# Attention and a two-layer feed-forward on one Trainium2 core: when the layout transfers are issued, and which engine subtracts in 2 of 18 steps

## Chip, cores and metric

One core of one Trainium2 chip runs the whole program. The metric is device time in microseconds of one execution; before the change three runs gave 998.31, 1001.68 and 1002.51 us, the median is 1001.68 us.

## What is computed

The reference, cut to what matters (4 batches, 8 heads, 1152 positions, head width 64; 2304 tokens, 512 to 2048 to 512):

```python
q_pool = q.reshape(B, H, S // 2, 2, D).mean(axis=3)
scores = scale * np.matmul(q_pool, k.transpose(0, 1, 3, 2))
scores = scores - np.max(scores, axis=-1, keepdims=True)
attn = np.exp(scores)
attn = attn / (np.sum(attn, axis=-1, keepdims=True) + 1e-09)
attn_out = np.matmul(attn, v)
x = attn_out.transpose(0, 2, 1, 3).reshape(B * S, H * D)
h = x @ w_in
r = np.maximum(h, 0.0)
out = (s * (r * r) + b) @ w_out
```

## The kernel before

The 32 heads are taken in 16 pairs. A head has 9 blocks of 128 keys, so a pair has 18 **steps**, numbered 0 to 17 here, and the attention 288. The feed-forward follows it in the last 417 us or so.

**A step.** `score_step` (line 480) makes the scores `s` of one block of keys against the head's 576 pooled queries: four matmuls on `kk` and `qq`. The kind of the step is read from the string `KIND`. In a "v" step ScalarE writes the exponential twice, once rounded (`ph`) and once in full, and VectorE subtracts them to `pl` (line 501). In a "g" step it is the same, but the full one goes to a buffer `pe` and GpSimd subtracts. In a "w" step (whole) there is one exponential, to `pe`, and nothing is subtracted. Three steps later `value_step` multiplies: for "v" and "g" six matmuls in rounded float32 (ph with vv, ph with vl, pl with vv, for two halves; lines 524, 526, 528), for "w" two matmuls in full float32 (pe with vf, line 518; each is two records in the trace). After a head's last block, `finish` lets ScalarE copy the sums out (lines 544 and 545, called clearing here), and the next head's first value matmuls need these banks. One or two matmuls `m` per step (line 456) find the maxima of the scores of a later pair.

**Preparing a pair.** For each head `load_v` fetches the values (`vf`), and `prep_v` lets GpSimd split them into `vv` and `vl`. For each pair `load_k` and `load_q` fetch keys and queries (`kraw`, `qraw`: 4 and 8 transfers), and `prep_pair` turns them: VectorE transposes, GpSimd adds (`qs`), rounds (`kh`, `qh`, `qz`) and subtracts (`kT`, `qT`). `lay` then issues five transfers for one head, two to `kk` and three to `qq`: the **layout transfers** ("l0" the first head, "l1" the second; lines 404 to 407). `shift` finds a head's maximum, and ScalarE sends it in two small transfers (`c` to `qq`, lines 471 and 472).

**What sets the order.** Each engine runs its instructions in the order written, and tables say at which step of a pair a piece is written: `PREP` for the pieces of preparation, `LR` for the k and q loads, `VS` for `prep_v`; the values are loaded at steps 3 and 12. Layouts, loads and results all go through SyncE's queue. In steps n % 18 == 4 from n = 166 on, weights of the feed-forward are fetched and, from pair 10 on, converted on ScalarE, VectorE and GpSimd (`conversions`, lines 163 to 180).

**Semaphores of the transfers.** The built program has eight for all transfers of SyncE and ScalarE, DMAHW0 to DMAHW7, given out in turn. A transfer waits until the one before it with the same semaphore has landed.

The line that the layouts' steps come from, and those that use it:

```python
            if p + 2 < NPAIR and n % 18 == PREP[0][1]:
                prep = prep_pair(p + 2)
            for name, at in PREP if n >= 8 else ():
                if n % 18 == at and name in prep:
                    prep.pop(name)()
```

Of the kernel before, what the change touches and what calls it, by code (L numbers as in the profile page):

```python
# [31 lines left out]
KB = 384  # L32


KIND = "vgvwvgvgw" * 2

PP = (("ka", 0), ("kb", 0), ("ha", 0), ("hb", 1), ("qs", 1), ("qt", 1), ("qm", 2), ("qh", 2), ("qz", 2), ("kl", 2), ("ql", 3), ("l0", 7))
PREP = (("qs", 9), ("ka", 10), ("kb", 11), ("ha", 11), ("qt", 12), ("hb", 12), ("kl", 12), ("qm", 13), ("qh", 13), ("qz", 13), ("ql", 14), ("l0", 0), ("l1", 8))
LR = 13
LD = 1  # L40
VS = (7, 16)
XT = (1, 2, 3, 4, 8)
# [10 lines left out]
def f32(ap):  # L53
    return ap.bitcast(F32)
# [3 lines left out]
def attention_moe_kernel(ctx: ExitStack, tc: tile.TileContext, q, k, v, w_in, w_out, s_in, b_in, out):  # L58
# [12 lines left out]
    NPAIR = NH // 2  # L71
# [138 lines left out]
    def hi_of(eng, out, in_):  # L210
        if eng is nc.scalar:
            nc.scalar.activation(out, in_, AF.Copy)  # L212
        else:
            eng.tensor_scalar(out=out, in0=in_, scalar1=1.0, scalar2=0.0, op0=ALU.mult, op1=ALU.add)  # L214
# [115 lines left out]
    qm = ap.tile([P, P], F32R, name="qm")  # L330
# [16 lines left out]
    def load_k(p):  # L347
        kraw[p] = ap.tile([P, NB, 32], F32, tag="kraw", name=f"kraw{p}")
        for r, b, h, c in quarters(p):
            nc.sync.dma_start(kraw[p][r], k[b, h, :, c].rearrange("(j t) i -> t j i", t=32))  # L350
# [11 lines left out]
    def load_v(hd):  # L362
        nc.sync.dma_start(vfs[hd % 2][:, :, 0:D], v[hd // H, hd % H].rearrange("(j p) d -> p j d", p=P))

    def prep_pair(p):

        kr, qr = kraw.pop(p), qraw.pop(p)
        kT = ap.tile([P, S], F32, tag="kT", bufs=2, name=f"kT{p}")
        qT = ap.tile([P, SQ], F32, tag="qT", bufs=2, name=f"qT{p}")
        qs = ap.tile([P, NBQ, 32], F32, tag="qs", name=f"qs{p}")  # L370
        kh = ap.tile([P, S], F32R, tag="kh", bufs=2, name=f"kh{p}")
        qh = ap.tile([P, SQ], F32R, tag="qh", bufs=2, name=f"qh{p}")
        krv = kr.rearrange("p j i -> p (j i)")
        lo, hi = slice(0, SQ), slice(SQ, S)

        def corner():
            assert holds.get("qm", -1) == p - 1
            for h in range(2):
                d = slice(h * D, (h + 1) * D)
                hi_of(nc.scalar, qm[d, d], qT[d, NT4 * P:])  # L380
            holds["qm"] = p

        def k_hi(part, last):
            hi_of(nc.scalar if p < 2 else nc.gpsimd, kh[:, part], kT[:, part])
            if last:
                khs[p] = kh

        def q_hi():
            hi_of(nc.scalar if p < 2 else nc.gpsimd, qh, qT)
            qhs[p] = qh  # L390

        def q_blocks():

            for h in range(2):
                r = slice(h * D, (h + 1) * D)
                hi_of(nc.scalar if p < 2 else nc.gpsimd, qzs[p % 2][r, h].rearrange("p (t m) -> p t m", t=NT4), qT[r, :NT4 * P].rearrange("p (m t) -> p t m", t=NT4))

        def lay(h):
            hd = 2 * p + h
            kk, qq = kks[hd % 3], qqs[hd % 3].rearrange("p i a n -> p i (a n)")  # L400
            r = slice(h * D, (h + 1) * D)
            ks = ((f32(kk[D:P, 0, :]), kT[r]), (f32(kk[0:D]), f32(kh[r]).unsqueeze(1).to_broadcast([D, 2, S])))
            for dst, src in ks[::-1] if hd == 0 else ks:
                nc.sync.dma_start(dst, src)
            nc.sync.dma_start(f32(qq[0:D, 0, :]), f32(qh[r]))
            nc.sync.dma_start(f32(qq[D:P, 0, :]), f32(qh[r]))
            nc.sync.dma_start(f32(qq[0:D, 1, :]), qT[r])
            holds["k", hd % 3] = hd

        return {  # L410
            "ka": lambda: nc.vector.transpose(out=kT[:, lo], in_=krv[:, lo]),
            "qs": lambda: (nc.vector if p < 2 else nc.gpsimd).tensor_tensor(out=qs, in0=qr[:, :, 0, :], in1=qr[:, :, 1, :], op=ALU.add),
            "kb": lambda: nc.vector.transpose(out=kT[:, hi], in_=krv[:, hi]),
            "ha": lambda: k_hi(lo, False),
            "qt": lambda: nc.vector.transpose(out=qT, in_=qs.rearrange("p j i -> p (j i)")),
            "hb": lambda: k_hi(hi, True),
            "qh": q_hi,
            "qz": q_blocks,
            "kl": lambda: nc.gpsimd.tensor_tensor(out=kT, in0=kT, in1=f32(kh), op=ALU.subtract),  # L419
            "ql": lambda: nc.gpsimd.tensor_tensor(out=qT, in0=qT, in1=f32(qh), op=ALU.subtract),  # L420
            "qm": corner,
            "l0": lambda: lay(0),
            "l1": lambda: lay(1),
        }
# [55 lines left out]
    def score_step(hd, j, kind):  # L480
        assert holds["k", hd % 3] == holds["c", hd % 3] == hd
        kk, qq = kks[hd % 3], qqs[hd % 3]
        ps = ps_s.tile([P, 2, 512], F32, tag="s", name=f"s{hd}_{j}")
        for a in range(2):
            for i in range(2):
                nc.tensor.matmul(ps[:, a, :HALF], kk[:, i, j * P:(j + 1) * P], qq[:, i, a], start=(i == 0), stop=(i == 1))  # L486
        if kind != "v":
            pe = late.tile([P, 2, HALF], F32, tag="pe", bufs=PE, name=f"pe{hd}_{j}")
        if kind == "w":
            nc.scalar.activation(pe, ps[:, :, :HALF], AF.Exp, scale=SCALE)  # L490
            prob[hd, j] = pe, None
            return
        ph = late.tile([P, 2, HALF], F32R, tag="ph", bufs=PB, name=f"ph{hd}_{j}")
        pl = late.tile([P, 2, HALF], F32R, tag="pl", bufs=PB, name=f"pl{hd}_{j}")
        nc.scalar.activation(ph, ps[:, :, :HALF], AF.Exp, scale=SCALE)  # L495

        full = ps[:, :, :HALF] if kind == "v" else pe
        nc.scalar.activation(full, ps[:, :, :HALF], AF.Exp, scale=SCALE)  # L498
        prob[hd, j] = ph, pl
        eng = nc.vector if kind == "v" else nc.gpsimd  # L500
        fresh.append(lambda: eng.tensor_tensor(out=pl, in0=full, in1=f32(ph), op=ALU.subtract))  # L501
# [92 lines left out]
    prep = prep_pair(0)  # L594
# [11 lines left out]
    for n in range(AHEAD):  # L606
# [3 lines left out]
        if n == 11:  # L610
            load_v(1)
            prep = prep_pair(1)
    nc.sync.dma_start(sb[:, 0:1], s_in.unsqueeze(0).to_broadcast([P, 1]))
    nc.sync.dma_start(sb[:, 1:2], b_in.unsqueeze(0).to_broadcast([P, 1]))

    moe = Moe()
    weights_a = conversions(wa, wstage, 0, SW[0], 1, STA)
    NS = NH * NJ

    for n in range(NS + LAG):  # L620
        hd, j = divmod(n, NJ)

        at = (n - LAG) % NJ if n >= LAG else None
        products = None
        units = iter(range((n + AHEAD) * NU // 18, (n + AHEAD + 1) * NU // 18) if n + AHEAD < NS else ())
        for part in ORD[at] if at is not None else "sff":
            if part == "s" and n < NS:
                score_step(hd, j, KIND[n % 18])
            elif part == "f":
                for u in units:  # L630
                    max_unit(u, ps_m, "m")
                    break
            elif part == "v":
                if products is None:
                    products = value_step(*divmod(n - LAG, NJ))
                next(products)
        for fn in fresh:
            fn()
        fresh.clear()
        if n < NS:  # L640
            p, h = divmod(hd, 2)
            for name, at in PP:
                if n == at:
                    prep.pop(name)()
            if n == LD:
                load_k(2)
                load_q(2)
            if p + 2 < NPAIR and n % 18 == PREP[0][1]:
                prep = prep_pair(p + 2)
            for name, at in PREP if n >= 8 else ():  # L650
                if n % 18 == at and name in prep:
                    prep.pop(name)()
            if p + 2 < NPAIR:
                if n % 18 == LR and p + 3 < NPAIR:
                    load_k(p + 3)
                    load_q(p + 3)
            if hd + 1 < NH:
                if j == LAG and hd >= 1:
                    load_v(hd + 1)
                if n % 18 in VS:  # L660
                    prep_v(hd + 1)
            if n == NS - 3 * NJ:
                moe.fetch(0)
            if n == NS - 2 * NJ:
                moe.split(0, 1)
            if (CB - n) % CP == 0 and 0 <= CB - n < 7 * CP:
                weights_a()
        tick()
# [79 lines left out]
```

## Time and profile before

| What | us |
|---|---|
| median of three runs | 1001.68 |
| the profiled execution | 1000.3 |
| its span in the trace | 998.4 |
| TensorE busy (matmuls) | 921.4 |
| VectorE, ScalarE, GpSimd busy | 630.1, 564.7, 549.8 |

The execution's own time is 1.9 us more than its span, and lies 1.4 us below the median. Busy times are sums over the span; matmuls overlap at their ends, so a busy TensorE is not one at its peak. The start of a step's first score matmul is the best clock of the attention: the 16 pairs begin at 22.1, 57.9, 92.5 and so on, pair 8 at 302.7, pair 10 at 370.8, pair 14 at 515.2.

### The profile page before, as it was taken

The page shows a single profiled execution, that of the slowest core. Times are in us where ns is not written, and L with a number is a line of the kernel's source. Part 1 is how long each engine was busy: PE and PEld are TensorE (multiplying, and loading weights), DVE is VectorE, ACT ScalarE, POOL GpSimd, SP SyncE. Part 2 cuts the span into 40 slices and gives each one's busy share as a digit, 9 for nine tenths or more (in the row PEclk, how much of TensorE's full clock was granted, in tenths as well). Part 3 has the DMA queues.
Part 4 walks back from the last instruction along what each step waited for, and adds up shares of the span by engine and source line. Part 5 has one row for each costly group of instructions (what it writes and reads, how often), then busy time and mean ns, then how long its engine had stood idle before and what let it go on. Part 6 is the DMA issues. An engine that isn't in the chain of part 4 may idle for free.

```text
span 998.4 us, 16537 instructions
## 1 busy us (share of the span) xinstructions
PE 921.4 (92%) x5776; PEld 821.1 (82%) x5776; DVE 630.1 (63%) x1168; ACT 564.7 (57%) x1086; POOL 549.8 (55%) x437
## 2 busy tenths in 40 slices
PE   5998988899899899888889998999999999999998
PEld 3887877788788788877778887789999899999997
DVE  5766776676676668668767556676767664334333
ACT  2776665666676667667667856564444443333332
POOL 7667647757755785786695766673534440010000
PEclk9999999999999999999999999999999999999999
DMA  8987865865686597578574135665354433222311
GB/s 151 174 160 138 173 130 94 175 146 105 131 169 129 103 192 162 108 155 179 108 165 118 46 110 166 201 218 163 127 169 127 148 106 106 64 67 89 99 43 43
DMA packets 255313, 131.18 MB, mean 131 GB/s; under 512 B 203776, under 2 KB 227328, under 8 KB 255232
## 3 DMA queue, kind: packets, MB, share of 16 engines
q1 hardware_dynamic: 244512, 129.62, 54.4%
q10 hardware_dynamic: 10720, 0.52, 0.7%
q8 instruction: 46, 0.75, 0.3%
q14 instruction: 35, 0.29, 0.1%
HBM read 68.68 MB, written 18.87 MB: 88 GB/s over the span
## 4 chain that ended last, share of the span: by engine, by line
PE 58%; POOL 13%; DMA 8%; ACT 8%; DVE 6%; issue 4%; ACTq 1%; SPq 0%; POOLq 0%; DVEq 0%
PE h L272 16%; PE y L299 16%; PE s L486 9%; PE o L524 4%; PE m L456 4%; POOL pl L501 4%; PE o L528 4%; PE o L526 3%; PE o L518 3%; POOL kT L419 2%; POOL qz L214 2%; DMA vf<-in_v_dram 2%; DMA kk<-kh 2%; ACT ph L495 2%; DMA wsto<-in_moe_w_out_dram 2%
## 5 line engine op out<-in xcount | busy, mean ns | idle before, releaser
L457 DVE TENSOR_REDUCE pm<-m 128x1 f32<-128x384 f32 x432 | 233.0, 550 | 128.8 <-PE m L456 124.6
L495 ACT ACTIVATE ph<-s 128x576 fp32r<-128x576 f32 x224 | 145.9, 651 | 133.7 <-PE s L486 114.1
L272 PE MATMUL h<-x,wih 128*128 128x256 f32 x1152 | 213.2, 283 | 6.2 <-DVE gl L286 3.9
L486 PE MATMUL s<-qq,kk 128*128 128x288 f32 x1152 | 213.8, 308 | 4.1 <-DVE pl L501 3.6
L272 PEld LDWEIGHTS h<-x,wih 128*128 128x128 f32 x1152 | 185.8, 189 | 21.2 <-DVE gl L286 3.5
L501 POOL TENSOR_TENSOR pl<-pe,ph 128x576 fp32r<-128x576 f32 x96 | 137.5, 1432 | 104.8 <-ACT pe L498 103.5
L486 PEld LDWEIGHTS s<-qq,kk 128*128 128x128 f32 x1152 | 174.7, 192 | 16.4 <-PE o L528 4.4
L272 PE MATMUL h<-x,wil 128*128 128x256 f32 x576 | 162.2, 282 | 0.0
L528 PE MATMUL o<-pl,vv 128*128 128x288 f32 x448 | 135.7, 303 | 27.4 <-POOL pl L501 27.4
L456 PE MATMUL m<-kh,qz 128*128 128x384 f32 x384 | 153.5, 409 | 5.9 <-DVE pm L457 5.8
L524 PE MATMUL o<-ph,vv 128*128 128x288 f32 x448 | 138.7, 310 | 12.0 <-issue 4.4
L253 POOL TENSOR_TENSOR x<-xr,x 128x1024 fp32r<-128x1024 f32 x27 | 64.8, 2401 | 152.6 <-ACT x L212 146.9
L280 DVE SCALAR_TENSOR_TENSOR h<-h,sb,r 128x256 f32<-128x256 f32 x144 | 70.2, 488 | 115.2 <-ACT r L289 115.2
L526 PE MATMUL o<-ph,vl 128*64 128x288 f32 x448 | 134.1, 299 | 5.4 <-POOL vl L431 5.2
L528 PEld LDWEIGHTS o<-pl,vv 128*128 128x128 f32 x448 | 85.7, 191 | 45.9 <-POOL pl L501 35.4
L289 ACT ACTIVATE r<-h 128x256 f32<-128x256 f32 x144 | 55.7, 387 | 111.0 <-PE h L272 111.0
L501 DVE TENSOR_TENSOR pl<-s,ph 128x576 fp32r<-128x576 f32 x128 | 96.3, 752 | 28.5 <-ACT s L498 21.3
L299 PE MATMUL y<-wol,gh 128*128 128x512 f32 x288 | 113.1, 393 | 0.0
L299 PE MATMUL y<-woh,gl 128*128 128x512 f32 x288 | 112.9, 392 | 0.0
L299 PE MATMUL y<-woh,gh 128*128 128x512 f32 x288 | 112.6, 391 | 0.0
L272 PEld LDWEIGHTS h<-x,wil 128*128 128x128 f32 x576 | 109.6, 190 | 0.0
L524 PEld LDWEIGHTS o<-ph,vv 128*128 128x128 f32 x448 | 85.6, 191 | 25.1 <-ACT l L545 8.0
(89 smaller groups left out, 1492.0 us busy)
## 6 DMA issues: line engine op xcount, KB each, us to landing
kk<-kh SPq DMA_DIRECT2D x32, 576.0 KB, 5.6
kraw<-in_k_dram SPq DMA_DIRECT2D x64, 144.0 KB, 3.7
vf<-in_v_dram SPq DMA_DIRECT2D x32, 288.0 KB, 4.8
kk<-kT SPq DMA_DIRECT2D x32, 288.0 KB, 3.3
qq<-qh SPq DMA_DIRECT2D x64, 144.0 KB, 5.6
xr<-xd SPq DMA_DIRECT2D x18, 512.0 KB, 4.0
qraw<-in_q_dram SPq DMA_DIRECT2D x122, 72.0 KB, 2.5
wsti<-in_moe_w_in_dram SPq DMA_DIRECT2D x16, 512.0 KB, 5.0
```

Of the source, the lines that this page charges most:

```text
L253: nc.gpsimd.tensor_tensor(out=xl, in0=xr, in1=f32(xh), op=ALU.subtract)
L272: nc.tensor.matmul(h[:, :TB], st[:, c, :], mv[:, c, :], start=(n == 0), stop=(n == 3 * NC - 1))
L280: nc.vector.scalar_tensor_tensor(out=t, in0=h[:, :TB], scalar=sb[:, 0:1], in1=r, op0=ALU.mult, op1=ALU.mult)
L299: nc.tensor.matmul(y[:, :DM], st[:, ts_], mv, start=(first and n == 0), stop=(last and n == 2))
L456: nc.tensor.matmul(ps[:, :KB], st, khs[p][:, e * KB:(e + 1) * KB], start=True, stop=True)
L457: nc.vector.tensor_reduce(out=pms[p][:, col, e:e + 1], in_=ps[:, :KB], axis=AX.X, op=ALU.max)
L486: nc.tensor.matmul(ps[:, a, :HALF], kk[:, i, j * P:(j + 1) * P], qq[:, i, a], start=(i == 0), stop=(i == 1))
L495: nc.scalar.activation(ph, ps[:, :, :HALF], AF.Exp, scale=SCALE)
L501: fresh.append(lambda: eng.tensor_tensor(out=pl, in0=full, in1=f32(ph), op=ALU.subtract))
L524: nc.tensor.matmul(o[:, :HALF], vv[:, j], ph[:, a], start=first, stop=False)
L526: nc.tensor.matmul(o[0:D, :HALF], vl[:, j], ph[:, a], start=False, stop=False)
L528: nc.tensor.matmul(o[:, :HALF], vv[:, j], pl[:, a], start=False, stop=last)
```

## The change

Two edits. In `KIND`, of nine steps the kinds are now v w v g v w v g w instead of v g v w v g v g w: of 18 steps 8 are "v" as before, 4 instead of 6 "g", 6 instead of 4 "w". The "g" steps are 3, 7, 12 and 16 instead of 1, 5, 7, 10, 14 and 16. In `PREP`, the layouts of the pair ahead are written at steps 4 and 13 instead of 0 and 8, and the k and q loads at step 14 instead of 13; a second dictionary, `lays`, keeps the layouts that fall after step 9, at which the next pair's preparation replaces `prep`.

```diff
-KIND = "vgvwvgvgw" * 2
+KIND = "vwvgvwvgw" * 2
...
-PREP = (("qs", 9), ("ka", 10), ("kb", 11), ("ha", 11), ("qt", 12), ("hb", 12), ("kl", 12), ("qm", 13), ("qh", 13), ("qz", 13), ("ql", 14), ("l0", 0), ("l1", 8))
-LR = 13
+PREP = (("qs", 9), ("ka", 10), ("kb", 11), ("ha", 11), ("qt", 12), ("hb", 12), ("kl", 12), ("qm", 13), ("qh", 13), ("qz", 13), ("ql", 14), ("l0", 4), ("l1", 13))
+LR = 14
...
+    lays = {}
...
-            if p + 2 < NPAIR and n % 18 == PREP[0][1]:
-                prep = prep_pair(p + 2)
-            for name, at in PREP if n >= 8 else ():
-                if n % 18 == at and name in prep:
-                    prep.pop(name)()
+            if n % 18 == PREP[0][1]:
+                lays = {k: prep[k] for k in ("l0", "l1") if k in prep}
+                prep = prep_pair(p + 2) if p + 2 < NPAIR else {}
+            for name, at in PREP:
+
+                ops = prep if name not in ("l0", "l1") or at < PREP[0][1] else lays
+                if n % 18 == at and name in ops and n >= 8:
+                    ops.pop(name)()
```

**SyncE, around the value load of a pair's second head** (pair 8; the number behind a name is its buffer's, and a row shows the semaphores that it waits for). Before, from the fifth q load on, and ScalarE's two sends of c that use DMAHW1 and DMAHW3:

```order
L358 DMA qraw_3595<-in_q_dram 32x18x32 [waits DMAHW0_49]
L358 DMA qraw_3595<-in_q_dram 32x18x32 [waits DMAHW1_49]
L358 DMA qraw_3595<-in_q_dram 32x18x32 [waits DMAHW2_49]
L358 DMA qraw_3595<-in_q_dram 32x18x32 [waits DMAHW3_49]
L404 DMA kk_94<-kT_3483 64x1152 [waits DMAHW4_49,PE_49,Pool_49]
L404 DMA kk_94<-kh_3486 64x2x1152 [waits DMAHW5_49,PE_49]
L405 DMA qq_97<-qh_3487 64x576 [waits DMAHW6_49,Pool_49]
L406 DMA qq_97<-qh_3487 64x576 [waits DMAHW7_49]
L407 DMA qq_97<-qT_3484 64x576 [waits DMAHW0_49,Pool_49]
L363 DMA vf_104<-in_v_dram 128x9x64 [waits DMAHW1_49,PE_49]
L471 DMA qq_99<-c_3752 1x128x4 [waits DMAHW1_49,DVE_49]
L472 DMA qq_99<-c_3752 1x64x1 [waits DMAHW3_49]
```

Now, from the third q load on; the two sends of c use DMAHW7 and DMAHW0:

```order
L358 DMA qraw_3491<-in_q_dram 32x18x32 [waits DMAHW6_49]
L358 DMA qraw_3491<-in_q_dram 32x18x32 [waits DMAHW7_49]
L358 DMA qraw_3491<-in_q_dram 32x18x32 [waits DMAHW0_49]
L358 DMA qraw_3491<-in_q_dram 32x18x32 [waits DMAHW1_49]
L358 DMA qraw_3491<-in_q_dram 32x18x32 [waits DMAHW2_49]
L358 DMA qraw_3491<-in_q_dram 32x18x32 [waits DMAHW3_49]
L363 DMA vf_104<-in_v_dram 128x9x64 [waits DMAHW4_49,PE_49]
L404 DMA kk_94<-kT_3358 64x1152 [waits DMAHW5_49,Pool_49]
L404 DMA kk_94<-kh_3361 64x2x1152 [waits DMAHW6_49]
L405 DMA qq_97<-qh_3362 64x576 [waits DMAHW0_49,Pool_49]
L471 DMA qq_99<-c_3615 1x128x4 [waits DMAHW7_49,DMAHW5_49,DVE_49]
L472 DMA qq_99<-c_3615 1x64x1 [waits DMAHW0_49]
```

The five layout transfers of the first head stood between the q loads and the value load, and now stand behind it. The sends of c come ahead of the q loads that use their semaphores: before, those were the sixth and the eighth; now they are the fourth and the fifth.

**GpSimd, the preparation of a pair** (pl is the subtraction of a "g" step; pl_1 and pl_5 before are those of steps 10 and 14, pl_3 now that of step 12, and pl_7 that of step 16). Before:

```order
L412 TENSOR_TENSOR qs_3485<-qraw_3168 128x576
L501 TENSOR_TENSOR pl_1_3497<-pe_1_3495,ph_1_3496 128x576
L214 TENSOR_SCALAR kh_3486<-kT_3483 128x576 x2
L419 TENSOR_TENSOR kT_3483<-kT_3483,kh_3486 128x1152
L214 TENSOR_SCALAR qh_3487<-qT_3484 128x576
L214 TENSOR_SCALAR qz_102<-qT_3484 64x512 x2
L501 TENSOR_TENSOR pl_5_3611<-pe_5_3609,ph_5_3610 128x576
L420 TENSOR_TENSOR qT_3484<-qT_3484,qh_3487 128x576
L501 TENSOR_TENSOR pl_7_3650<-pe_7_3648,ph_7_3649 128x576
L214 TENSOR_SCALAR vv_105<-vf_103 128x9x64
```

Now:

```order
L412 TENSOR_TENSOR qs_3360<-qraw_3080 128x576
L214 TENSOR_SCALAR kh_3361<-kT_3358 128x576
L501 TENSOR_TENSOR pl_3_3415<-pe_3_3413,ph_3_3414 128x576
L214 TENSOR_SCALAR kh_3361<-kT_3358 128x576
L419 TENSOR_TENSOR kT_3358<-kT_3358,kh_3361 128x1152
L214 TENSOR_SCALAR qh_3362<-qT_3359 128x576
L214 TENSOR_SCALAR qz_102<-qT_3359 64x512 x2
L420 TENSOR_TENSOR qT_3359<-qT_3359,qh_3362 128x576
L501 TENSOR_TENSOR pl_7_3526<-pe_7_3524,ph_7_3525 128x576
L214 TENSOR_SCALAR vv_105<-vf_103 128x9x64
```

One subtraction of step 12 stands between the two halves of kh where one of step 10 stood ahead of both, and none is left between qz and qT.

## Rows read from the trace of the kernel before

**Rows 1.** The page: TensorE's busy time and share of the span with the other engines', and the chain of work that ended last, by engine.

```profile
PE 921.4 (92%) x5776; PEld 821.1 (82%) x5776; DVE 630.1 (63%) x1168; ACT 564.7 (57%) x1086; POOL 549.8 (55%) x437
...
PE 58%; POOL 13%; DMA 8%; ACT 8%; DVE 6%; issue 4%; ACTq 1%; SPq 0%; POOLq 0%; DVEq 0%
```

**Rows 2.** Busy time by stage: pairs 1 to 9, and pairs 10 to 13. A row has the stretch, its length, then each engine's busy time and count, TensorE's granted clock, the DMA share and GB/s.

```profile
57.90:370.80 312.90, 280.07 (x1793) 249.61 (x1792) 214.84 (x388) 206.89 (x378) 209.66 (x171) 0.99 0.71 141
370.80:515.20 144.40, 128.00 (x799) 112.51 (x798) 106.53 (x188) 97.83 (x181) 106.86 (x87) 0.99 0.70 146
```

**Rows 3.** TensorE's timeline in pair 8 (302.7 to 337.8) and the first steps of pair 9: start, duration, line, output and inputs, count, and in brackets the idle time before it with what ended it. Each row of L486 is the score matmuls of one step: step 9 at 318.40, 10 at 319.89, 11, 12, 13 at 326.71, 14 at 329.38, 17 at 334.40, 0 at 337.79, 2 at 340.96, 3 and 4.

```profile
318.40 0.69 PE L486 MATMUL s<-qq,kk 128*128 128x288 f32 x4
...
319.36 0.29 PE L528 MATMUL o<-pl,vv 128*128 128x288 f32 x1
...
319.89 0.69 PE L486 MATMUL s<-qq,kk 128*128 128x288 f32 x4
...
321.56 0.69 PE L486 MATMUL s<-qq,kk 128*128 128x288 f32 x4
...
323.02 0.91 PE L486 MATMUL s<-qq,kk 128*128 128x288 f32 x4
...
324.51 0.40 PE L524 MATMUL o<-ph,vv 128*128 128x288 f32 x1 [0.41 <-POOL vv L214]
...
326.71 0.70 PE L486 MATMUL s<-qq,kk 128*128 128x288 f32 x4
...
329.38 0.69 PE L486 MATMUL s<-qq,kk 128*128 128x288 f32 x4
...
334.40 0.69 PE L486 MATMUL s<-qq,kk 128*128 128x288 f32 x4
...
337.15 0.40 PE L528 MATMUL o<-pl,vv 128*128 128x288 f32 x1 [1.62 <-POOL pl L501]
...
337.79 0.69 PE L486 MATMUL s<-qq,kk 128*128 128x288 f32 x4
...
340.96 0.69 PE L486 MATMUL s<-qq,kk 128*128 128x288 f32 x4
...
342.81 0.69 PE L486 MATMUL s<-qq,kk 128*128 128x288 f32 x4
...
345.13 0.69 PE L486 MATMUL s<-qq,kk 128*128 128x288 f32 x4
```

**Rows 4.** GpSimd's timeline in pair 8, from the subtraction of step 7 to that of step 16, columns as in rows 3.

```profile
317.15 1.43 POOL L501 TENSOR_TENSOR pl<-pe,ph 128x576 fp32r<-128x576 f32 x1 [0.54 <-ACT pe L498]
323.79 0.67 POOL L214 TENSOR_SCALAR vv<-vf 128x576 fp32r<-128x576 f32 x1 [5.21 <-DMA vf<-in_v_dram]
...
327.29 1.41 POOL L501 TENSOR_TENSOR pl<-pe,ph 128x576 fp32r<-128x576 f32 x1
328.67 1.31 POOL L214 TENSOR_SCALAR kh<-kT 128x576 fp32r<-128x576 f32 x2
330.06 2.66 POOL L419 TENSOR_TENSOR kT<-kT,kh 128x1152 f32<-128x1152 f32 x1
...
335.70 1.40 POOL L501 TENSOR_TENSOR pl<-pe,ph 128x576 fp32r<-128x576 f32 x1
337.06 1.43 POOL L420 TENSOR_TENSOR qT<-qT,qh 128x576 f32<-128x576 f32 x1
338.44 1.43 POOL L501 TENSOR_TENSOR pl<-pe,ph 128x576 fp32r<-128x576 f32 x1
```

**Rows 5.** SyncE's queue in pair 8: start of the issue, its duration on the queue, the transfer and the count; the first row is the sixth to eighth q load.

```profile
310.64 1.39 SPq L358 DMA_DIRECT2D qraw<-in_q_dram  x3
312.15 0.47 SPq L404 DMA_DIRECT2D kk<-kT  x1
...
316.95 0.84 SPq L407 DMA_DIRECT2D qq<-qT  x1
317.89 0.59 SPq L363 DMA_DIRECT2D vf<-in_v_dram  x1
```

**Rows 6.** The waits of SyncE's queue over the whole span: who waited for what, us in total, times, the longest.

```profile
SPq L358 <- DMA qq<-c: 124.9, 15, 11.5
```

**Rows 7.** ScalarE's timeline in pair 8: the second send of c after step 3, the two exponentials of step 11, and the one of step 12.

```profile
309.27 0.61 ACTq L472 DMA_DIRECT2D qq<-c  x1
...
322.29 0.65 ACT L495 ACTIVATE ph<-s 128x576 fp32r<-128x576 f32 x1 [0.47 <-PE s L486]
322.84 0.65 ACT L498 ACTIVATE s<-s 128x576 f32<-128x576 f32 x1
...
325.09 0.65 ACT L490 ACTIVATE pe<-s 128x576 f32<-128x576 f32 x1
```

**Rows 8.** All instructions that touch the tile vf, last line: time from the issue of its loads to their landing.

```profile
DMA to landing us min/median/max: 3.1/4.8/7.0
```

**Rows 9.** Pair 10, in which weights are converted: two conversions on GpSimd's timeline, and on TensorE's the score matmuls of steps 9 and 10.

```profile
400.16 1.27 POOL L174 TENSOR_TENSOR wRi<-wRi,wabi 128x512 f32<-128x512 f32 x1
407.12 1.29 POOL L177 TENSOR_TENSOR wAi<-wAi,wih 128x512 f32<-128x512 f32 x1
...
386.53 0.69 PE L486 MATMUL s<-qq,kk 128*128 128x288 f32 x4
389.37 0.69 PE L486 MATMUL s<-qq,kk 128*128 128x288 f32 x4
```

## The prediction, made before the changed kernel was run

> **What bounds the kernel now.** I read the page first: TensorE is busy for 92% of the span, yet on the chain that ended last it holds only 58%, GpSimd 13% and DMAs 8% [rows 1]. So the question is where TensorE stands still. The table by stage answers it: pairs 1 to 9 of the attention take 312.9 us with TensorE busy for 280.07, pairs 10 to 13 (in which weights of the second layer are converted as well) 144.4 with 128.00 [rows 2]. After the attention the change touches nothing, and I leave those 417 us alone.
>
> TensorE's own timeline gives the pace without waits [rows 3]. The score matmuls of two steps start 1.49 us apart when one maximum matmul lies between (318.40 to 319.89) and 1.67 with two (319.89 to 321.56). A whole ("w") step costs 1.85 instead of 1.67 (340.96 to 342.81): 0.18 more. The step in which a head's sums are cleared away takes 2.32 (342.81 to 345.13), 0.83 above its kind; that happens twice in a pair. A pair of 18 steps with four whole ones is then 9 x 1.67 + 9 x 1.49 + 4 x 0.18 + 2 x 0.83 = 30.8 us. Pairs 1 to 9 take 312.9 / 9 = 34.8, so **about 3.95 us per pair are waits**. In the pair shown they are at three places: step 12 (323.02 to 326.71, 3.69, with TensorE released by the vv copy), step 13 (2.67 instead of 1.49) and step 17 (334.40 to 337.79, 3.39 instead of 1.49, released by GpSimd's subtraction pl).
>
> GpSimd explains all three [rows 4]. It runs in order. It finished pl of step 7 at 318.58, then stood until the values had landed and began vv at 323.79. Behind vv lie vl, qs, pl of step 10, kh, kT, qh and qz without a gap, and only then pl of step 14 (335.70 to 337.10), which TensorE took up at 337.15. So the late values start a burst that is late to its end.
>
> Why are the values late? SyncE's queue says it [rows 5]: the last three q loads were issued from 310.64, then came five layout transfers (312.15 to 317.8), and the values only at 317.89. The q loads had been held: SyncE spent 124.9 us on such waits for the small transfers of c [rows 6]. Here ScalarE issued c at 309.27 [rows 7] and SyncE went on 1.4 us later. Each DMA waits for the one that used its semaphore before, as the order of the rows with their waits shows, and in the program before, the sixth and eighth q load follow c.
>
> **The change, part by part.**
>
> Layouts behind the values. In the order of the changed program the values follow the q loads directly, and the fourth and fifth q load follow c, so five loads instead of three come after the release. Three loads took 1.5 us (310.64 to 312.15) [rows 5], so five take 2.5: the values go out at about 313.2 instead of 317.89. A value load lands 3.1 to 7.0 us after its issue, 4.8 in the middle [rows 8]; with 4.8 it lands at 318.0, about when GpSimd is through with pl at 318.58 [rows 4]. Even 7.0 (320.2) leaves vv and vl ready before 323. The waits at steps 12 and 13 go. What covers the layouts: the first head's are issued from 314, and are wanted at the next pair's first step, more than 17 us later. The second head's now stand behind the second value load and wait for the other c; the five take some 6 us and land before the next pair's middle, where they are wanted. Of the moved DMAs none is added, and k and q loads stay behind them as before, so both are costed at nothing. If that cover failed, all DMAs of a pair would slide by the same delay, and q loads are needed only at step 9.
>
> Whole instead of GpSimd. Two steps in 18, 32 in all, lose a subtraction on GpSimd (1.38 us from start to start [rows 4], off the path where GpSimd waits anyway) and one exponential on ScalarE (not the bound). TensorE pays 32 x 0.18 = **5.8 us**, 0.36 per pair. The Trainium skill speaks against it: FP8 and Floating Point Precision, section TensorE Precision Notes, has true FP32 take four passes through the array, against three products of one pass here. An estimate by it: the 1.49 us step holds eleven matmuls of about 0.135, two passes more are 0.27, 8.7 us in all, and the end 2.9 us later than by the row. The measured step, 0.18, decides.
>
> Order of the burst. The subtractions now belong to steps 3, 7, 12 and 16. Step 14 is whole, so the wait at step 17 goes (1.9 us). But pl of step 12 stands inside the burst and holds it, and pl of step 16 comes after all of it. Pl of step 12 wants two exponentials: before, the single one ran from 325.09 to 325.74, and the second of two starts 0.55 after the first (322.29, 322.84) [rows 7], so it is ready at 326.29, 3.27 after step 12 began. From there pl 1.38, one kh 0.70 (half of 1.39), kT, qh and qz 5.64 (330.06 to 335.70), qT 1.38 and pl 1.43 [rows 4]: 10.53, ending at 13.8 after step 12's start. TensorE wants it at step 19: four even steps, three odd, one clearing and two whole ones, 6.68 + 4.47 + 0.83 + 0.36 = 12.34, and 0.96 into the step (318.40 to 319.36) [rows 3], 13.3. So **a new wait of 0.5 us** stands at the next pair's step 1. Bounds: none, if ScalarE clears the head 0.5 us sooner; 2.5, if GpSimd's start slips by two more exponentials and a clearing.
>
> Sum for pairs 1 to 9: 30.8 + 0.36 + 0.5 = 31.7 against 34.8, 3.1 x 9 = 27.8 us. Pairs 10 to 13 take 36.1 each. There two conversions on GpSimd (400.16, 407.12; 1.25 each) come before pl of step 16, so the new wait is 3.0; a wait of 1.35 at step 9 stays (386.53 to 389.37, 2.84 instead of 1.49), which VectorE's part of the conversion makes [rows 9]. 31.2 + 1.35 + 3.0 = 35.5, a gain of 0.6 x 4 = 2.3. Pairs 0, 14 and 15 pay 1.1 for their whole steps and win about as much at pair 0's steps 12 to 14: nothing. Together 30.1. The profiled execution took 1000.3 us, 1.4 below the median of 1001.68; 1000.3 - 30.1 = 970.2, as a median **971.5 us**.
>
> **The rivals.**
>
> A wait takes the removed one's place. If pl of step 12 starts 1 us later than I read, step 19 waits 1 us more in each of 13 pairs: 13 us, 984.5. For it: the burst has no slack there. Against: 325.09 stands in the trace.
>
> The values stay late, and the change doesn't do what it says. If the hold by c moved, the values landing at 323.7 as now, step 12 keeps 0.9 us, the burst begins 0.8 later and step 19 waits 1.4: 31.2 + 0.9 + 1.4 = 33.5, 1.3 x 9 + 2.3 = 14 us gained, 987.7. Against it stands the order of the rows.
>
> Slower. The same place, GpSimd's in-order burst held by pl of step 12, turns the sign: 30 us over 13 pairs are lost again once pl's input comes 2.3 us later than read, as when ScalarE, which clears the head in the same step, falls behind by a clearing and two exponentials. At 3 us the end is 1001.7 + 39 - 30 = 1010.5. Against: ScalarE has one exponential less twice per pair.
>
> Better. If step 19 doesn't wait, neither in plain pairs nor in those with conversions, 9 x 0.5 + 4 x 3 = 16.5 us more: 955.
>
> Four passes at full price: 974.4, by the skill's page named above. The whole steps in the trace, 0.18 apart, speak against it.
>
> **How the numbers follow.** My forecast 0.54; the late start by about 1 us 0.16; values still late 0.07; better 0.07; four passes 0.04; all of these are faster by over 0.5% (5 us, about what a measurement of this kernel can tell from no change): 0.88. A start so late that it eats the gain 0.06, beyond it 0.06. The range of 958 to 990 holds the forecast with its bounds of the step-19 wait, the two partial cases and most of the better one. The forecast alone is 962 to 981.
>
> **What would show it.** Right: attention ends about 30 us sooner; SyncE issues the values before the layouts, some 2.5 us after the held q load; GpSimd no longer waits for the values; TensorE's waits at steps 12, 13 and 17 are gone and a short one stands at step 1, of some 3 us after pairs with conversions; TensorE's value matmuls on pe are 384 records instead of 256. Wrong: a pair still near 34 us, or GpSimd idle before pl of step 12 for long while step 1 waits over 2 us in plain pairs.

## The result, and the profile after

| | before | after |
|---|---|---|
| median of four runs, us | 1000.86 | 975.11 (973.74 to 976.95) |
| ratio, 95% interval | | 0.9746 (0.9718 to 0.9774) |
| pairs 1 to 9, us | 312.9 | 289.2 |
| pairs 10 to 13, us | 144.4 | 141.8 |
| pairs 14 and 15, to the last step's scores, us | 62.5 | 64.1 |
| from there to the end, us | 420.7 | 422.0 |

The change made the kernel 2.5% faster; 971.5 us were predicted, 958 to 990 as the range. The profiled execution of after took 976.95 us (span 975.2), the slowest of its four, so the traces differ by 23.2 us where the medians differ by 25.75.

The page of after, busy times and the chain, beside [rows 1]:

```profile
PE 922.3 (95%) x5712; PEld 821.4 (84%) x5712; DVE 627.0 (64%) x1168; ACT 545.9 (56%) x1054; POOL 507.5 (52%) x405
...
PE 67%; ACT 12%; POOL 7%; DVE 5%; DMA 3%; issue 3%; ACTq 1%; SPq 0%; DVEq 0%; POOLq 0%
```

TensorE does as much and fills 95% of the span instead of 92; on the chain GpSimd fell from 13 to 7% and the DMAs from 8 to 3%, while **ScalarE rose from 8 to 12%**. Hold on to that.

Busy time by stage, columns as in [rows 2]: pairs 1 to 9, then 10 to 13.

```profile
58.10:347.30 289.20, 279.07 (x1758) 250.03 (x1756) 212.65 (x388) 196.10 (x360) 186.99 (x154) 1.00 0.74 151
347.30:489.10 141.80, 130.00 (x783) 113.62 (x781) 108.11 (x189) 93.41 (x172) 95.89 (x78) 0.98 0.73 151
```

Of the 23.7 us that pairs 1 to 9 gained, TensorE's waiting gave nearly all: 312.90 less 280.07 is 32.8 before [rows 2], 289.20 less 279.07 is 10.1 now. GpSimd's waits for the values over the whole span (us in total, times, the longest), before, after, and in experiment 11 below:

```profile
POOL vv L214 <- DMA vf<-in_v_dram: 60.5, 14, 6.4
POOL vv L214 <- DMA vf<-in_v_dram: 6.4, 6, 2.5
POOL vv L214 <- DMA vf<-in_v_dram: 2.3, 1, 2.3
```

SyncE's queue in pair 8 (its first step began at 283.17) answers to [rows 5]; first row: the fourth to eighth q load.

```profile
291.30 2.47 SPq L358 DMA_DIRECT2D qraw<-in_q_dram  x5
293.88 0.44 SPq L363 DMA_DIRECT2D vf<-in_v_dram  x1
294.42 0.57 SPq L404 DMA_DIRECT2D kk<-kT  x1
295.04 0.62 SPq L404 DMA_DIRECT2D kk<-kh  x1
295.76 0.87 SPq L405 DMA_DIRECT2D qq<-qh  x1
296.68 2.63 SPq L406 DMA_DIRECT2D qq<-qh  x1
...
304.63 0.61 SPq L404 DMA_DIRECT2D kk<-kT  x1
309.82 0.62 SPq L404 DMA_DIRECT2D kk<-kh  x1
```

The values leave 2.58 us after the release of the q loads. GpSimd, in the same pair, answers to [rows 4]: subtraction of step 7, then vv with no wait in its brackets; the wait is now ahead of the subtraction of step 12; the last row is that of step 16.

```profile
297.83 1.41 POOL L501 TENSOR_TENSOR pl<-pe,ph 128x576 fp32r<-128x576 f32 x1 [1.65 <-ACT pe L498]
299.21 0.67 POOL L214 TENSOR_SCALAR vv<-vf 128x576 fp32r<-128x576 f32 x1
...
307.15 1.41 POOL L501 TENSOR_TENSOR pl<-pe,ph 128x576 fp32r<-128x576 f32 x1 [2.81 <-ACT pe L498]
...
316.32 1.43 POOL L501 TENSOR_TENSOR pl<-pe,ph 128x576 fp32r<-128x576 f32 x1
```

TensorE's scores of steps 12, 13 and 14 answer to [rows 3], and ScalarE between them to [rows 7]: four clearings up to 305.85, the two exponentials of step 12, the two sends of c.

```profile
303.80 0.91 PE L486 MATMUL s<-qq,kk 128*128 128x288 f32 x4
...
307.12 0.80 PE L486 MATMUL s<-qq,kk 128*128 128x288 f32 x4 [0.56 <-ACT pe L498]
308.68 0.91 PE L486 MATMUL s<-qq,kk 128*128 128x288 f32 x4
```

```profile
305.44 0.41 ACT L545 ACTIVATE l<-o 64x288 f32<-64x288 f32 x1
305.87 0.65 ACT L495 ACTIVATE ph<-s 128x576 fp32r<-128x576 f32 x1
306.42 0.65 ACT L498 ACTIVATE pe<-s 128x576 f32<-128x576 f32 x1
306.88 0.49 ACTq L471 DMA_DIRECT2D qq<-c  x1
307.47 0.90 ACTq L472 DMA_DIRECT2D qq<-c  x1
308.41 0.65 ACT L495 ACTIVATE ph<-s 128x576 fp32r<-128x576 f32 x1 [1.35 <-PE o L518]
```

Step 12 is 3.32 us long. The waits at steps 13 and 17 are gone, and the wait that the prediction put at the next pair's step 1 isn't there:

```profile
318.09 0.29 PE L528 MATMUL o<-pl,vv 128*128 128x288 f32 x1
```

In its place TensorE stands 0.56 before the scores of step 13, for ScalarE's second exponential of step 12: in the built program the scores of step 13 are given the bank (the piece of memory for scores) that step 12's exponentials read. In pairs 11 to 14 step 1 does wait, here pair 11, TensorE, and ahead of it GpSimd's conversion and its subtraction of step 16:

```profile
385.50 0.40 PE L528 MATMUL o<-pl,vv 128*128 128x288 f32 x1 [1.83 <-POOL pl L501]
```

```profile
382.80 1.29 POOL L177 TENSOR_TENSOR wAi<-wAi,wih 128x512 f32<-128x512 f32 x1
384.05 1.39 POOL L501 TENSOR_TENSOR pl<-pe,ph 128x576 fp32r<-128x576 f32 x1
```

### The profile page after: what moved, and what is told of

Its sections match the earlier page's. It is cut to its first block, busy times and chain, and to the rows that moved or that the text cites. A ratio compares the mean times of both kernels' runs of the same rounds, so it can differ in the third digit from the quotient of the medians.

```text
span 975.2 us, 16173 instructions
## 1 busy us (share of the span) xinstructions
PE 922.3 (95%) x5712; PEld 821.4 (84%) x5712; DVE 627.0 (64%) x1168; ACT 545.9 (56%) x1054; POOL 507.5 (52%) x405
## 4 chain that ended last, share of the span: by engine, by line
PE 67%; ACT 12%; POOL 7%; DVE 5%; DMA 3%; issue 3%; ACTq 1%; SPq 0%; DVEq 0%; POOLq 0%
PE h L272 18%; PE y L299 17%; PE s L486 12%; PE o L518 5%; PE m L456 5%; PE o L524 4%; PE o L528 4%; PE o L526 4%; ACT ph L495 3%; ACT xu L544 2%; ACT l L545 2%; ACT s L498 2%; POOL pl L501 1%; DVE pm L457 1%; DMA wsto<-in_moe_w_out_dram 1%
## 5 line engine op out<-in xcount | busy, mean ns | idle before, releaser
L457 DVE TENSOR_REDUCE pm<-m 128x1 f32<-128x384 f32 x432 | 230.6, 549 | 112.8 <-PE m L456 106.9
L486 PE MATMUL s<-qq,kk 128*128 128x288 f32 x1152 | 217.6, 311 | 10.9 <-ACT pe L498 7.8
L495 ACT ACTIVATE ph<-s 128x576 fp32r<-128x576 f32 x192 | 125.2, 652 | 132.4 <-PE s L486 109.8
L486 PEld LDWEIGHTS s<-qq,kk 128*128 128x128 f32 x1152 | 175.6, 191 | 27.2 <-ACT pe L498 11.0
L501 POOL TENSOR_TENSOR pl<-pe,ph 128x576 fp32r<-128x576 f32 x64 | 91.5, 1429 | 141.8 <-ACT pe L498 131.2
L456 PE MATMUL m<-kh,qz 128*128 128x384 f32 x384 | 156.9, 418 | 3.2 <-DVE pm L457 3.1
L524 PE MATMUL o<-ph,vv 128*128 128x288 f32 x384 | 119.0, 310 | 7.8 <-issue 4.8
L518 PE MATMUL o<-pe,vf 128*128 128x288 f32 x384 | 126.0, 412 | 0.0
L528 PE MATMUL o<-pl,vv 128*128 128x288 f32 x384 | 113.6, 296 | 7.3 <-POOL pl L501 7.3
L501 DVE TENSOR_TENSOR pl<-s,ph 128x576 fp32r<-128x576 f32 x128 | 96.2, 752 | 30.9 <-ACT s L498 24.7
L526 PE MATMUL o<-ph,vl 128*64 128x288 f32 x384 | 113.6, 296 | 0.0
L283 ACT ACTIVATE gh<-h,sb 128x256 fp32r<-128x256 f32 x144 | 68.0, 473 | 64.6 <-DVE h L280 64.3
```

What stands on the lines that cost most here:

```text
L456: nc.tensor.matmul(ps[:, :KB], st, khs[p][:, e * KB:(e + 1) * KB], start=True, stop=True)
L457: nc.vector.tensor_reduce(out=pms[p][:, col, e:e + 1], in_=ps[:, :KB], axis=AX.X, op=ALU.max)
L518: nc.tensor.matmul(o[:, :HALF], vfs[hd % 2][:, j], ph[:, a], start=first, stop=last)
L524: nc.tensor.matmul(o[:, :HALF], vv[:, j], ph[:, a], start=first, stop=False)
L526: nc.tensor.matmul(o[0:D, :HALF], vl[:, j], ph[:, a], start=False, stop=False)
L528: nc.tensor.matmul(o[:, :HALF], vv[:, j], pl[:, a], start=False, stop=last)
```

## The experiments

All in one table; each ratio is to the kernel before on the same chip. The stages run from the first score matmul of pair 1, of 10 and of 14, so divide by 9 and 4 for a pair. A plain pair is one of pairs 1 to 9, which convert no weights.

| kernel | median us | ratio, 95% interval | pairs 1-9 | pairs 10-13 |
|---|---|---|---|---|
| after (the change) | 975.11 | 0.9718 to 0.9774 | 289.2 | 141.8 |
| 1 layouts alone | 986.07 | 0.9842 to 0.9875 | 303.9 | 137.3 |
| 2 kinds alone | 982.51 | 0.9797 to 0.9855 | 297.1 | 140.9 |
| 3 step 14 for step 12 | 967.36 | 0.9652 to 0.9685 | 288.1 | 136.2 |
| 4 ten whole steps | 970.95 | 0.9691 to 0.9720 | 294.8 | 133.5 |
| 5 layouts, c on SyncE | 967.00 | 0.9652 to 0.9681 | 278.1 | 137.7 |
| 6 late conversion | 966.49 | 0.9652 to 0.9680 | 288.8 | 135.7 |
| 7 third, c on SyncE | 966.35 | 0.9646 to 0.9678 | 281.2 | 137.3 |
| 8 third, spread conversion | 962.83 | 0.9612 to 0.9648 | 287.7 | 131.6 |
| 9 old kinds, combined | **953.23** | 0.9505 to 0.9541 | 278.2 | 133.1 |
| 10 new kinds, combined | 963.15 | 0.9608 to 0.9641 | 286.6 | 135.8 |
| 11 before, c on SyncE alone | 960.58 | 0.9577 to 0.9614 | 281.0 | 137.7 |
| 12 layouts, kh last | 968.23 | 0.9662 to 0.9709 | 287.4 | 137.8 |

**1 and 2: the change taken apart.**

```diff
-KIND = "vwvgvwvgw" * 2
+KIND = "vgvwvgvgw" * 2
```

That is 1, in the kernel after; 2 is the opposite edit in the kernel before. The kinds differ in six of 18 steps (1, 3, 5, 10, 12 and 14); what is two fewer is the steps that GpSimd subtracts.

> The kernel after with the old kinds (six g, four w): only the layout transfers and the k and q loads are moved. Theory (the late values made all three waits): with the values there at step 9, GpSimd's burst starts some 4 us earlier even with its six subtractions, pl of step 14 is through about when TensorE wants it (in pair time 29.6 against 29.9, from the changed kernel's rows), and no pl of step 12 stands in the burst; pairs 1 to 9 take 31.0 to 31.5 us each against 32.1 after, pairs 10 to 13 35 to 36.5, and the whole 968 to 977. Rival (the prediction's part on the burst: the wait at step 17 goes because step 14 is whole): 1 to 2 us stay at step 17, plain pairs take 32.2 to 33, the whole is 980 to 986.

> The kernel before with the new kinds alone (four g, six w); the layouts stay ahead of the values. Theory: the values still land about 5 us late, TensorE keeps a wait at step 12 or 13 and GpSimd's burst ends late at step 1 of the next pair; 33.5 us for a plain pair, 985 to 990 in all. Rival (the fewer subtractions of GpSimd are what gains): 972 to 980, plain pairs below 32.7.

Neither came as either theory had it. In the first TensorE has no wait for the values, and none at step 17, whose scores and those of the next pair's step 0 start 1.50 us apart:

```profile
327.65 0.69 PE L486 MATMUL s<-qq,kk 128*128 128x288 f32 x4
...
329.15 0.69 PE L486 MATMUL s<-qq,kk 128*128 128x288 f32 x4
```

Yet a plain pair takes 33.8 us. It waits at step 14 instead, where no theory looked. ScalarE's timeline in pair 8 (first step at 295.9), from the single exponential of step 12 to the first of step 13, and SyncE's first transfers of the second head's layout beside it:

```profile
318.26 0.65 ACT L490 ACTIVATE pe<-s 128x576 f32<-128x576 f32 x1
319.26 0.49 ACTq L471 DMA_DIRECT2D qq<-c  x1
319.85 2.20 ACTq L472 DMA_DIRECT2D qq<-c  x1
322.09 0.65 ACT L495 ACTIVATE ph<-s 128x576 fp32r<-128x576 f32 x1 [3.19 <-PE o L524]
```

```profile
317.01 0.61 SPq L404 DMA_DIRECT2D kk<-kT  x1
317.68 0.62 SPq L404 DMA_DIRECT2D kk<-kh  x1
324.45 0.47 SPq L405 DMA_DIRECT2D qq<-qh  x1
```

```profile
324.22 0.76 PE L486 MATMUL s<-qq,kk 128*128 128x288 f32 x4 [1.82 <-DVE pl L501]
```

The second send of c holds ScalarE's queue for 2.20 us, the exponentials of step 13 stand behind it, VectorE's subtraction behind those, and TensorE (last fence) waits 1.82 us for the score bank at the end of step 14. In after, SyncE's kh transfer goes out only behind the sends (309.82 against 306.88), since there it shares a semaphore with the first (landed at 309.80), and the second send takes 0.90. The kinds alter how the program's transfers fall in order, and that is what the first experiment lost, as 5 and 12 below test. In the second the values stay late, as expected (GpSimd waits 61.3 us for them over the span), at 33.0 us a plain pair.

**3: step 14 instead of step 12 to GpSimd.**

```diff
-KIND = "vwvgvwvgw" * 2
+KIND = "vwvgvwvgw" + "vwvwvgvgw"
```

> The kernel after with the second head's kinds v w v w v g v g w instead of v w v g v w v g w: as many of each, but step 12 whole and step 14 subtracted by GpSimd. Theory: in plain pairs what is left of waiting is ScalarE's second exponential of step 12 behind the clearing (0.55 us), and in pairs 10 to 14 pl of step 12, which holds GpSimd's burst 2.8 us; both go, pl of step 14 is in time. Plain pairs 31.5, pairs 10 to 13 34 to 35, the whole 962 to 968. Rival (the excess of step 12 is the clearing alone, and the burst is bound by its length): plain pairs stay at 32.1, or step 17 waits again, 974 to 982.

The whole came as the theory said, the plain pairs as the rival: 32.0. Step 12 lost its 0.55, and step 14 took 0.4 of it back: TensorE there waits 0.33 us (pair 8) for VectorE's subtraction of step 13, whose exponentials stand behind the sends. Of the 7.7 us gained, 5.6 are in pairs 10 to 13: GpSimd's last subtraction begins 1.75 us sooner (in pair 10, at 35.0 us of the pair instead of 36.8), step 1 waits less, and TensorE's clock (last section) doesn't fall. That step 12 had held the burst, as the theory has it, isn't shown by this: in pair 10 GpSimd stands 1.54 us for VectorE's transposes where it had stood 1.94 for step 12, and 1.54 of the 1.75 us are there already at vv.

**4: ten whole steps.**

```diff
-KIND = "vwvgvwvgw" * 2
+KIND = "vwvwvwvww" * 2
```

> The kernel after with v w v w v w v w w for both heads: ten whole steps, no subtraction on GpSimd. Theory (a whole step costs TensorE 0.18 to 0.20 more, and GpSimd's subtractions make the waits of pairs 10 to 14): plain pairs 31.9 to 32.1, pairs 10 to 13 32.9 to 33.5 without the wait at step 1, the whole 962 to 968. Rival (a whole step costs 0.27, four passes): plain pairs 32.7 to 32.9 and the whole 972 to 977.

Mixed: plain pairs took 32.8 us and the whole 970.95, both above the theory, and pairs 10 to 13 took 33.4, as it said. The price comes out against the third, which has the same wait at step 14 and four whole steps fewer: (294.8 - 288.1) / 9 / 4 = 0.19 us. What I had missed was the wait at step 14, the same 0.4 as in the third (2.3 us for the step, against 1.9 in the tenth).

**5 and 12: the send taken off ScalarE, and the large transfer put behind it.** Both start from the first, with the old kinds.

The fifth, the second send likewise; then the twelfth, whose last two lines stand behind the three transfers to qq:

```diff
-            nc.scalar.dma_start(f32(row[D:D + 1, :NT4 * P]), f32(c[:, full]))
+            nc.sync.dma_start(f32(row[D:D + 1, :NT4 * P]), f32(c[:, full]))
```

```diff
-            for dst, src in ks[::-1] if hd == 0 else ks:
+            for dst, src in ks[::-1] if hd == 0 else ks[:1]:
...
+            if hd:
+                nc.sync.dma_start(*ks[1])
```

> The first experiment's kernel (layouts moved, old kinds: 986 us, 33.8 us for a plain pair, of which 2 us are a wait at step 14) with the two small sends of c on SyncE's queue instead of ScalarE's. Theory: there the second send of c of step 13 took ScalarE's queue 2.2 to 2.6 us, since the first head's kk transfer of kh was in flight, and the exponentials of step 13 stood behind it; with the send gone from ScalarE, step 14 waits 0.2 us or less, the half clock behind that wait goes too, and plain pairs take 31.0 to 31.8 with the old kinds: 962 to 971 in all. Rival (it is GpSimd's longer burst or VectorE that holds step 14; the send is only beside it): step 14 still waits over 1.5 us, 33 us for a plain pair, 980 to 988.

> The first experiment's kernel (layouts moved, old kinds, c sent by ScalarE: 986 us, step 14 waits 2 us) with the large transfer of kh as the last of a head's five layout transfers instead of the second; by its semaphore it then follows the first send of c. Theory (the transfer that is issued second behind kh's takes over 2 us to issue, on either queue, and in the first experiment that was ScalarE's second send of c): the send takes 0.6 to 1.2 us, step 14 waits at most 0.8, plain pairs 31.3 to 32.2, the whole 968 to 976. Rival (any layout transfers ahead of c make the send long): the send keeps 2 us, 33 us or more a plain pair, 980 to 988.

Both came as the theory had them (in the twelfth step 14 waits up to 1.0 us, where at most 0.8 was expected), both with **the old kinds faster than after**. In the fifth a plain pair takes 30.9 us, the pace without waits of the prediction (30.8). Its first pair lost 8.5 us, since the first head's c there stands in SyncE's queue behind eight loads and five layout transfers: it is ready at 20.1, issued at 29.01 and landed at 31.79, and TensorE stands for 8.82 us at the first scores. In the twelfth the order on ScalarE is the same as in the first, and only the transfer of kh is behind the sends:

```profile
303.34 0.65 ACT L492 ACTIVATE pe<-s 128x576 f32<-128x576 f32 x1
304.35 0.49 ACTq L473 DMA_DIRECT2D qq<-c  x1
304.94 0.86 ACTq L474 DMA_DIRECT2D qq<-c  x1
305.84 0.65 ACT L497 ACTIVATE ph<-s 128x576 fp32r<-128x576 f32 x1 [1.85 <-DVE pm L459]
```

0.86 instead of 2.20, with four other layout transfers ahead of it and kh issued at 307.86: the large one matters, not their number.

**6 and 8: the conversions.**

```diff
-STA = (0, 4, 4, 4, 6, 9, 11, 13)
+STA = (0, 4, 4, 4, 6, 9, 13, 14)
```

That is 6, in the kernel after; 8 is the third with `STA = (0, 1, 2, 3, 4, 12, 13, 14)`.

> The kernel after with the fourth and fifth GpSimd part of a weight conversion two and one steps later (steps 17 and 18 instead of 15 and 17), so behind pl of step 16. Nothing else. Theory: in pairs 10 to 14 pl of step 16 is through 1.25 us sooner, the wait at step 1 falls from 2.0 to 0.8 us and the half clock behind it (pairs 11 and 13) goes: 35.45 to about 34 us a pair, 968 to 970 in all. Rival (the wait follows ScalarE or the burst, not that conversion): no change, 974 to 976.

> The third experiment's kernel with the parts of a weight conversion spread: VectorE's three at steps 5, 6 and 7 instead of all at 8, GpSimd's three at steps 16 to 18 instead of 13, 15 and 17. Theory: in pairs 10 to 13 the waits at steps 9 (0.86, VectorE's three), 17 (0.46) and 1 (0.85) go, 34.1 to about 32.2 us each: 958 to 961 in all. Rival (those waits are the burst's length and VectorE's reductions, whatever the order): 965 to 969.

The sixth came as the theory said: one conversion of 1.29 us moved behind the subtraction of step 16, and in pair 11 TensorE's wait fell from 1.83 to

```profile
383.06 0.40 PE L528 MATMUL o<-pl,vv 128*128 128x288 f32 x1 [0.84 <-POOL pl L501]
```

and 6.1 us of 8.6 were gained in pairs 10 to 13, the falls of the clock behind that wait (last section) among them. The eighth gained 4.6 of the 7.6 hoped for there: the waits at 17 and 1 went, that of step 9 only moved to steps 6 and 7.

**7: the third with c on SyncE,** by the edit of the fifth.

> The third experiment's kernel (967 us, 32.0 us for a plain pair, 0.6 of it a wait at step 14 behind ScalarE's sends) with the sends of c on SyncE's queue. Theory: ScalarE's queue is free for the exponentials of step 13, plain pairs take 31.3 to 31.5, and 9 to 13 pairs gain 0.5 us each: 959 to 963. Rival (SyncE's queue then holds values or loads behind c): vv late, a wait at steps 12 and 13 is back, 968 to 980.

Plain pairs took 31.2 us, about as expected; the whole missed the theory by 3 us or more, since the first pair lost 8 us as in the fifth. Beside the fifth it prices two whole steps: (281.2 - 278.1) / 9 / 2 = 0.17 us.

**9 and 10: both kinds with the sends out of the way.** The layouts moved, STA as in 8, and

```diff
-            nc.scalar.dma_start(f32(row[D:D + 1, :NT4 * P]), f32(c[:, full]))
+            q = nc.scalar if hd < 2 else nc.sync
+            q.dma_start(f32(row[D:D + 1, :NT4 * P]), f32(c[:, full]))
```

> The layouts moved, the old kinds, the sends of c on SyncE's queue from the second pair on (the first pair's two heads keep ScalarE's queue, where the fifth experiment lost 8.5 us), and the parts of a weight conversion spread as in the eighth. Theory: 30.9 us for a plain pair as in the fifth, no 8.5 us at the start, pairs 10 to 13 at 31.7 to 32.2 instead of 34.4: 947 to 953 in all. Rival (pairs 10 to 13 are bound by GpSimd with its six subtractions): 34 us there, 957 to 960.

> As the ninth, with the change's kinds (four g, six w), the only difference between the two. Theory (with the sends off ScalarE the new kinds bring nothing in plain pairs and cost two whole steps and the second exponential of step 12): plain pairs 31.3 to 31.8 against 30.9, the whole 2 to 8 us above the ninth. Rival (GpSimd's shorter burst is worth it): equal or up to 5 us below the ninth.

The only difference is `KIND`, and **the change's kinds cost 9.9 us**, more than expected: 8.4 in pairs 1 to 9, 2.7 in 10 to 13. In plain pairs stands the wait that the prediction had put at step 1. Tenth, the subtraction of step 16 of pair 7 taken up in pair 8:

```profile
283.08 0.40 PE L529 MATMUL o<-pl,vv 128*128 128x288 f32 x1 [0.43 <-POOL pl L502]
```

It makes the step 0.70 longer than one of its kind. In this program step 13 doesn't wait for step 12's bank: its scores start 2.60 us after those of step 12 (pair 8), before the second exponential of step 12, which ran from 303.59 to 304.24.

```profile
300.98 0.91 PE L487 MATMUL s<-qq,kk 128*128 128x288 f32 x4
...
303.58 0.69 PE L487 MATMUL s<-qq,kk 128*128 128x288 f32 x4
```

The ninth is the fastest here, 4.8% below before; in pairs 10 to 13 I had hoped for 32 us a pair, and it took 33.3.

**11: the sends alone, in the kernel before.** The edit of 9, nothing else.

> The kernel before, with one edit that the change does not contain: the sends of c on SyncE's queue from the second pair on; layouts ahead of the values as before, old kinds. Theory (the late values are a matter of the held q loads as much as of the layouts): in SyncE's order the q loads and layouts now go out without waiting for c and the values right behind c, so the values land in time, plain pairs take 31 to 31.5, pairs 10 to 13 34 to 35, the whole 957 to 964. Rival (the layouts ahead of the values alone make them late): waits at steps 12 and 13 stay, 33 us or more a plain pair, 975 to 990.

As the theory said: this one edit, which the change doesn't contain, gained 40.2 us, where the change gained 25.75. From pair 2 on a plain pair takes 30.9 us, with the layouts ahead of the values and the old kinds. SyncE's queue, pair 9 (first step at 307.5):

```profile
304.03 4.67 SPq L358 DMA_DIRECT2D qraw<-in_q_dram  x8
308.81 0.49 SPq L404 DMA_DIRECT2D kk<-kT  x1
...
314.23 0.68 SPq L407 DMA_DIRECT2D qq<-qT  x1
314.99 0.56 SPq L472 DMA_DIRECT2D qq<-c  x1
315.61 0.60 SPq L473 DMA_DIRECT2D qq<-c  x1
316.30 0.54 SPq L363 DMA_DIRECT2D vf<-in_v_dram  x1
```

All eight q loads go without a hold, and the values leave 8.8 us into the pair, before the change 15.2 (317.89 in a pair that began at 302.7 [rows 5]), after it 10.7. The sends also leave ScalarE's queue here; that the gain comes from the values is read from GpSimd's waits for them (60.5 us before, 2.3 now, see the result), and no run separates the two.

## Why the prediction came out, and where it did not

**Late values: right.** The values went out 2.58 us behind the held q load (2.5 predicted), and GpSimd's waits for them fell from 60.5 us over the span to 6.4 (61.3 in the second experiment, which has the layouts ahead of them). But the layouts were only one part of the cause: without the hold by c they can stay ahead (11).

**The step that failed: "Step 14 is whole, so the wait at step 17 goes (1.9 us)."** With the old kinds and the values in time there is no wait at step 17 in plain pairs (1, 5, 9, 11); the earlier burst alone removes it. The kinds gained all the same, 11 us from experiment 1 to after (14.7 in pairs 1 to 9, less 4.5 lost in pairs 10 to 13), by something the prediction never priced: they put the second head's kh transfer behind ScalarE's sends. The prediction followed the sends only as something that holds SyncE; ScalarE was "not the bound", and the time for which a send holds ScalarE's queue entered no term. Where that is cured otherwise, the same kinds cost 9.9 us (9, 10). So the near hit of the whole is in part luck: the prediction gave the kinds a net 1.0 us a plain pair (1.9 at step 17, less 0.36 and 0.5), and they brought 1.6 at step 14, where it hadn't looked.

**A whole step at 0.18: right.** 0.19 and 0.17 by experiments 4 and 7. The estimate of 0.27, worked out from the four passes of the Trainium skill (FP8 and Floating Point Precision, section TensorE Precision Notes), was too high. The trace doesn't speak against four passes, but against the price that the estimate gave to one: in after, the two records of a whole matmul start 0.24 us apart, 0.12 for each of four passes if a record holds two, where the estimate took 0.135, the distance of separate matmuls. Eight times 0.12 less six times 0.13 is 0.18.

**The wait of 0.5 at step 1: right for GpSimd, wrong for TensorE.** GpSimd's part was read rightly: the subtraction of step 12 began 3.35 us after its step (3.27 predicted), and that of step 16 was through 13.95 after it (13.8). But the prediction, which saw that step 12 has two exponentials behind the clearing, used that only for GpSimd. TensorE waits for the second too (0.56), through the bank, so it reaches the matmul of step 1 at 14.3 instead of 13.3 and finds the subtraction ready. In experiment 10, whose program gives step 13 another bank, step 12 is 2.6 us long instead of 3.3, and the wait at step 1 is there. So 14.3 stands where the prediction had 13.3 and a wait of 0.5, and a plain pair took 32.1 us instead of 31.7: 23.7 measured of 27.8, the mis-sized term of the sum.

**Pairs 10 to 13: right by size, 35.45 against 35.5, otherwise made up, and so luck.** The prediction put a wait of 3.0 at step 1 and one of 1.35 at step 9 in each of the four. Step 1 waits 2.0 to 2.3, and in only three of them (the fourth such wait falls in pair 14), and step 9 about 0.9; but in pairs 11 and 13 the clock fell behind the wait (below). Experiment 6 shows that the conversion ahead of the last subtraction makes about 1 us of the wait.

**Costed at nothing:** pairs 14 and 15 took 1.6 us more. In pair 14 step 1 waits as in 11 to 13 (1.5 more than before), and step 14 took 1.6 more, since ScalarE's second send took 2.49 us at step 13, behind the layout of pair 15; steps 0 and 9 gave 0.8 each back. The rest took 1.3 more, which no experiment looked at; in the twelve experiments it took 419.2 to 421.9. The sum of 30.1 stands against 23.2 by the traces and 25.75 by the medians.

Of the rivals none took over. The slower one had named the right place, ScalarE in the step that clears, and a wrong consequence.

## What to carry to other kernels

A transfer issued from a compute engine's queue is an instruction in that engine's order: price its issue by the rows in which it runs behind other transfers, not by the row in which it runs alone. When two edits come together, measure each alone; here the one that looked like the cause of a gain worked only by moving a transfer, and costs time once that is done directly. Look first for what holds the queue (here a shared semaphore behind c), before reordering what stands in it.

## What the runs showed of the hardware

**An issue may take four times as long.** The transfer issued second behind kh's took 2.63 us on SyncE's queue (after, 296.68, above) and 2.20 on ScalarE's (experiment 1), where a send alone takes 0.61 [rows 7]. It was so each time in pairs 1 to 9 of these two kernels: behind kh's issue the next took 0.49 to 1.13 us, and the one after it 2.15 to 2.71, on whichever queue. The Trainium skill (Perfetto Trace Analysis, section DMA Instruction — HWDGE) says that the profiled time of such an issue holds the wait for a descriptor generator that two sequencers share, and the making of the descriptors, with a buffer that can fill. The trace agrees that an issue on one queue stretches behind a transfer of the other; which of these it waits for no run here shows.

**The clock fell behind short waits, not behind each.** In after, pair 11, TensorE had waited 1.83 us and worked 0.9; then its granted clock was 0.50 of full, the lower of its two levels, for 3.4 us:

```profile
385.50:386.40 0.90, 0.90 (x6) 0.90 (x7) 0.00 (x0) 0.63 (x1) 0.90 (x2) 0.98 1.10 173
386.40:389.80 3.40, 3.40 (x12) 2.81 (x11) 0.67 (x2) 2.42 (x6) 2.29 (x2) 0.50 0.07 13
```

Pairs 11 and 13, with the fall, took 36.6 and 36.9 us, pair 12, with a wait of 1.71 us and no fall, 34.9. In experiment 1 it fell in the same way behind waits of 1.86 us in pair 3 and 2.27 in pair 7, and stayed full behind 1.98 in pair 6. So a wait that costs 2 us may cost 4, and its length alone doesn't decide; what does is open.
